# Moving the decay of a linear-attention state from GpSimd to ScalarE, with sums over each head's own columns

## Chip, cores, metric

The kernel runs on one core of one Trainium2 chip. The metric is the device time of one execution in microseconds, as the median of several runs. The engines of the core are TensorE (PE, with its weight loads as PEld), VectorE (DVE), ScalarE (ACT), GpSimd (POOL) and SyncE (SP, which issues the DMAs here).

## What is computed

Three layers one after the other: a gated linear attention, a layer that mixes tokens with cosine and sine of a projection, and a gated convolution layer. The change touches only the first.

```python
B, H, S, D = 4, 8, 768, 48
state = zeros(B, H, D, D)
for t in range(S):
    state = alpha[:, :, t, :, None] * state + einsum('bhd,bhe->bhde', k[:, :, t], v[:, :, t])
    y[:, :, t] = einsum('bhd,bhde->bhe', q[:, :, t], state)
x = y as (B, S, H * D)
theta = x @ w_theta                       # then cos, sin of theta times x, mixed over tokens
u = x + w_tok_r @ (x * cos(theta)) + w_tok_i @ (x * sin(theta))
u = u + relu(u @ w_ch)
h = relu(u @ w_in); out = (h * sigmoid(conv3(h, conv_w))) @ w_out
```

## The kernel before

The recurrence is computed in chunks of 128 tokens, 6 chunks for each of 4 batches, 24 in all (index `ci`, chunk in its batch `c`). Rows of the tiles are head dimensions: two heads lie on one set of partitions, head j of a pair on rows 64j to 64j+47, and the 4 pairs (`NP`) lie side by side.

For each chunk, `a_prep` (L238) makes running products of alpha with two scans on VectorE (L246, L251, into the one buffer `fbt`), copies the total decay of the chunk per row into `ftot` (L254, ScalarE), squares everything for an overflow test (L257, ScalarE, which must have read `fbt` before the next scan may write it) and multiplies queries and keys by the running products (L260, VectorE). `a_score` (L263) transposes the keys (`kps`, TensorE), multiplies keys with queries (`sc`), copies scores to `pt` (L278, ScalarE), masks them (L279, GpSimd) and copies the transposed keys to `kt` (L283, ScalarE). `a_y` (L286) computes the output `y` of the chunk from `pt` and the values, and, for c > 0, from the state `Sp`; ScalarE copies it to `x` (L303). For c < 5 it then computes the outer products `kv` of keys and values over the chunk (L309), adds the old state (L313, VectorE, into `tst`), and multiplies by the total decay `nft` of the next chunk into the other state tile `Sn` (L321, GpSimd, two products, one for each set of rows). For c = 0 there is no old state, and ScalarE copies `kv` instead (L318). `a_xt` transposes x and ScalarE copies it to `u` (L338).

`kv` is computed for a whole pair of heads against the values of both (96 columns), though only the blocks of a head with itself are wanted; the rest is never read, since the products at L321 go over each head's own columns only.

Around this runs other work. Weights come in as 8-byte words and VectorE decodes them (L117 to L119) and splits them (L75). `a_theta` makes cosine and sine (L364 to L369) and splits them into `zh` and `zl`; `m_mix` multiplies them with the token weights (`yps`, TensorE). In the first batch attention, theta and loading run together; the attention of batch b+1 is then woven, chunk by chunk, with the first half of the mixing of batch b, and the theta of batch b+1 with the second half. After the attention of the last batch (about 260 us) come theta, mixing, and the two later layers.

Which instruction an engine issues next is fixed when the program is built: a planner simulates the engines and, on each, puts the instruction first that is ready by its simulation and comes earliest in the program. On the chip each engine then follows that order, whatever is ready. `behind` (L80) adds an order without a wait: the squares are issued behind the score, key, x and u copies made so far.

Of the kernel before, what the change touches and what calls it, by code (L numbers as in the profile page):

```python
# [8 lines left out]
F32 = mybir.dt.float32  # L9
# [5 lines left out]
AF = mybir.ActivationFunctionType  # L15
ALU = mybir.AluOpType
PSUM = bass.MemoryType.PSUM

P = 128
B, H, S, D = 4, 8, 768, 48  # L20
DM = H * D
DFF = 1024
NP = H // 2
# [23 lines left out]
def tile_gated_linear_attention__then__spectral_moe__then__conv_gate(  # L47
# [17 lines left out]
    def mm(o, lhsT, rhs, start, stop):  # L65
        nc.tensor.matmul(o, lhsT, rhs, start=start, stop=stop, skip_group_check=True)  # L66
# [34 lines left out]
    def body(top, slow):  # L101
# [46 lines left out]
        with ExitStack() as ph1:  # L148
# [37 lines left out]

            onehot = acon.tile([P, 5, SEG], BF16, name="onehot")
            starts = acon.tile([P, 4, SEG], F32, name="starts")
            Sst = [acon.tile([P, NP, 2 * D], F32, name=f"S{i}") for i in range(2)]
            magic = acon.tile([P, 1], F32, name="magic")  # L190
            halfpi = acon.tile([P, 1], F32, name="halfpi")
            wth_p = apool("wth", 2, side="right")
# [6 lines left out]
            nc.vector.memset(onehot, 0.0)  # L199
            nc.vector.memset(onehot[:, :, 0:1], 1.0)  # L200
            nc.vector.memset(starts, 0.0)
            for t in Sst:
                nc.gpsimd.memset(t, 0.0)
            nc.gpsimd.memset(magic, MAGIC)
            nc.gpsimd.memset(halfpi, math.pi / 2)

# [31 lines left out]
            def a_prep(ci):  # L238
                at, qt, vt = raw.pop(ci)
                qr = qt[:, 0:CW]  # L240
                kr = qt[:, CW : 2 * CW]
                fbt = sc_p.tile([P, 2 * AW + 6], F32, tag="fbt", name="fbt")
                bf = fbt[:, AW + 1 : 2 * AW + 2]
                of = onehot.rearrange("p a t -> p (a t)")
                ftot = att.tile([P, 4], F32, tag="ftot", name="ftot")
                nc.vector.tensor_tensor_scan(  # L246
                    bf[:, AW:0:-1], at[:, AW:0:-1], of[:, AW:0:-1], 0.0, ALU.mult, ALU.add
                )
                tots = bf[:, 1 : AW + 1].rearrange("p (a t) -> p a t", a=4)[:, :, 0]
                nc.vector.reciprocal(starts[:, :, 0], tots)  # L250
                nc.vector.tensor_tensor_scan(  # L251
                    fbt[:, :AW], at[:, :AW], starts.rearrange("p a t -> p (a t)"), 0.0, ALU.mult, ALU.add
                )
                nc.scalar.copy(ftot, tots)  # L254
                fl = fbt[:, 1 : 2 * AW + 5].rearrange("p (b t) -> p b t", b=2)[:, :, :AW]
                sink = at[:, : AW - 1].bitcast(BF16).rearrange("p (b t) -> p b t", b=2)
                sq = nc.scalar.activation(sink, fl[:, :, : AW - 1], AF.Square, accum_out=bacc[:, ci : ci + 1])  # L257
                behind(sq, ("pt", "kt", "x", "u"))
                q4 = qt.rearrange("p (b a t) -> p b a t", b=2, a=4)
                nc.vector.tensor_tensor(q4, q4, fl.rearrange("p b (a t) -> p b a t", a=4)[:, :, :, :P], ALU.mult)  # L260
                prep[ci] = (qr.rearrange("p (a t) -> p a t", a=4), kr.rearrange("p (a t) -> p a t", a=4), ftot, vt)

            def a_score(ci):  # L263
                qh, kh, ftot, vt = prep[ci]
                kt = None
                if ci % NC < NC - 1:
                    kps = ps_a.tile([P, 4, P], F32, tag="a", name="kps")
                    for p in range(NP):
                        nc.tensor.transpose(kps[:, p, :], kh[:, p, :], ident)
                scs = [ps_a.tile([P, NP, P], F32, tag="a", name="sc") for _ in range(2)]  # L270
                for p in range(NP):
                    for j in range(2):
                        r = slice(64 * j, 64 * j + D)
                        mm(scs[j][:, p, :], kh[r, p, :], qh[r, p, :], True, True)
                pts = []
                for j in range(2):
                    pt = att.tile([P, NP, P], F32, tag="pt", name="pt")
                    marks["pt"] = nc.scalar.copy(pt, scs[j])  # L278
                    nc.gpsimd.affine_select(pt, pt, [[0, NP], [1, P]], ALU.is_ge, 0.0, base=0, channel_multiplier=-1)  # L279
                    pts.append(pt)  # L280
                if ci % NC < NC - 1:
                    kt = att.tile([P, 4, P], F32, tag="kt", name="kt", bufs=1)
                    marks["kt"] = nc.scalar.copy(kt, kps)  # L283
                scored[ci] = (pts, kt)

            def a_y(ci):  # L286
                qh, kh, ftot, vt = prep.pop(ci)
                pts, kt = scored.pop(ci)
                c = ci % NC
                Sp, Sn = Sst[ci % 2], Sst[(ci + 1) % 2]  # L290
                y = ps_a.tile([P, DM], F32, tag="a", name="y")
                halves = [slice(64 * i, 64 * i + 64) for i in range(2)]
                for p in range(NP):
                    for j in range(2):
                        h = 2 * p + j
                        for t in halves:
                            mm(y[t, h * D : (h + 1) * D], pts[j][:, p, t], vt[:, h * D : (h + 1) * D], h == 0, c == 0)
                if c > 0:
                    for p in range(NP):
                        for t in halves:  # L300
                            mm(y[t, p * 96 : p * 96 + 96], qh[:, p, t], Sp[:, p, :], False, True)
                x = x_p.tile([P, DM], F32, tag="x", name="x")
                marks["x"] = nc.scalar.copy(x, y)  # L303
                xs[ci] = x
                if c < NC - 1:
                    kv = ps_a.tile([P, NP, 2 * D], F32, tag="a", name="kv")
                    for p in range(NP):
                        for t in halves:
                            mm(kv[t, p, :], kt[:, p, t], vt[:, p * 96 : p * 96 + 96], p == 0, True)  # L309
                    nft = prep[ci + 1][2]  # L310
                    if c > 0:
                        tt = att.tile([P, NP, 2 * D], F32, tag="tst", name="tst", bufs=1)
                        nc.vector.tensor_tensor(tt[:112], Sp[:112], kv[:112], ALU.add)  # L313
                    else:
                        tt = Sn
                        for j in range(2):
                            r = slice(64 * j, 64 * j + D)
                            nc.scalar.copy(Sn[r, :, j * D : (j + 1) * D], kv[r, :, j * D : (j + 1) * D])  # L318
                    for j in range(2):
                        r = slice(64 * j, 64 * j + D)  # L320
                        nc.gpsimd.tensor_tensor(  # L321
                            Sn[r, :, j * D : (j + 1) * D],
                            tt[r, :, j * D : (j + 1) * D],
                            nft[r].unsqueeze(2).to_broadcast([D, NP, D]),
                            ALU.mult,
                        )

            def a_xt(ci):
                b, c = divmod(ci, NC)
# [407 lines left out]
```

## Time and profile before

| | |
|---|---|
| median of 3 runs | 577.38 us (576.98 to 578.29) |
| profiled execution | 575.62 us |
| its span | 573.9 us |
| TensorE matmuls | 550.9 us busy (96%) |
| TensorE weight loads | 514.3 us (90%) |
| VectorE | 455.1 us (79%) |
| ScalarE | 336.0 us (59%) |
| GpSimd | 90.8 us (16%) |

The span runs from the first to the last instruction of the profiled execution. Busy shares are averages over stages with different limits, so the rows further down are taken stage by stage. A line of code can be that of a helper: all plain matmuls have L66, the splits L74 (the cast, ScalarE) and L75 (the difference, VectorE).

### The profile page before, as it was taken

Reading aid. Unit: us, or ns where it says so; the run is one execution under the profiler, and the core shown is the slowest. Engines: PE = TensorE matmul, PEld = TensorE weight load, DVE = VectorE, ACT = ScalarE, POOL = GpSimd, SP = SyncE. Lnnn points to the kernel's source line nnn. Section 1 sums busy time; section 2 is a strip of 40 time slices with the busy share of each in tenths; the row PEclk is TensorE's granted clock in tenths of the full one; section 3 lists DMA queues with packets and bytes.
Section 4 is the critical chain, followed back from the end, with each engine's and each line's share of the span. In section 5 each row is a group of like instructions: output and inputs, shape, how many; then the busy total and the mean of one; then the engine's idle time right before and its main releaser. Section 6 shows DMA issues by size and latency. Waiting matters only on the chain.

```text
span 573.9 us, 10776 instructions
## 1 busy us (share of the span) xinstructions
PE 550.9 (96%) x4317; PEld 514.3 (90%) x4317; DVE 455.1 (79%) x682; ACT 336.0 (59%) x685; POOL 90.8 (16%) x99
## 2 busy tenths in 40 slices
PE   6888989999999999999999999899999999999996
PEld 3766879877999999999999999799999999999995
DVE  7999998999767674642747999987888888898780
ACT  3566666457844476443742346567767766676661
POOL 2465414440154101440000000000000000000000
PEclk9699999999999999999999999999999999999998
DMA  8556544673044300400013333401053443647001
GB/s 323 182 166 200 189 143 139 203 265 102 15 139 140 125 2 15 140 15 1 1 55 138 111 111 111 164 1 42 14 193 118 145 147 115 198 138 243 17 30 46
DMA packets 25402, 66.59 MB, mean 116 GB/s; under 512 B 2560, under 2 KB 8704, under 8 KB 24960
## 3 DMA queue, kind: packets, MB, share of 16 engines
q1 hardware_dynamic: 25344, 65.82, 34.9%
q8 instruction: 36, 0.59, 0.4%
q14 instruction: 22, 0.18, 0.1%
HBM read 61.10 MB, written 4.72 MB: 115 GB/s over the span
## 4 chain that ended last, share of the span: by engine, by line
PE 70%; DVE 16%; DMA 7%; issue 2%; ACT 2%; POOL 2%; SPq 1%; DVEq 0%; POOLq 0%; ACTq 0%
PE yps L66 18%; PE ops L66 17%; PE hps L66 15%; PE th L66 5%; PE y L66 4%; PE cps L66 3%; PE sc L66 3%; DVE stage L118 2%; DMA stage<-in_w_in_dram 2%; DMA stage<-in_w_tok_dram 2%; DVE stage L117 2%; DVE stage L119 2%; PE kv L66 2%; DMA stage<-in_w_out_dram 1%; DMA stage<-in_w_theta_dram 1%
## 5 line engine op out<-in xcount | busy, mean ns | idle before, releaser
L66 PE MATMUL yps<-wtok,zh 128*128 128x384 f32 x576 | 152.6, 343 | 1.3 <-ACT zh L74 1.3
L66 PEld LDWEIGHTS yps<-wtok,zh 128*128 128x128 f32 x576 | 104.4, 189 | 5.0 <-ACT zh L74 1.6
L66 PE MATMUL hps<-x,win 128*128 128x386 f32 x576 | 107.7, 339 | 0.0
L66 PE MATMUL ops<-wout,g 128*128 128x384 f32 x576 | 106.9, 338 | 0.0
L66 PEld LDWEIGHTS hps<-x,win 128*128 128x128 f32 x576 | 102.3, 189 | 0.4
L66 PEld LDWEIGHTS ops<-wout,g 128*128 128x128 f32 x576 | 101.6, 188 | 0.4
L66 PE MATMUL yps<-wtok,zl 128*128 128x384 f32 x288 | 96.7, 341 | 0.8 <-DVE zl L75 0.8
L279 POOL TENSOR_SCALAR_AFFINE_SELECT pt<-pt 128x512 f32<-128x512 f32 x48 | 55.0, 1166 | 151.1 <-ACT pt L278 151.0
L66 PEld LDWEIGHTS yps<-wtok,zl 128*128 128x128 f32 x288 | 54.3, 189 | 2.0 <-DVE zl L75 1.0
L246 DVE TENSOR_TENSOR_SCAN fbt<-a_t,onehot 128x516 f32<-128x516 f32 x24 | 29.5, 1229 | 23.2 <-ACT a_t L257 21.3
L75 DVE TENSOR_TENSOR g<-cv,g 128x384 fp32r<-128x384 f32 x64 | 35.5, 556 | 12.2 <-ACT g L74 11.2
L561 ACT ACTIVATE cv<-cv 128x384 f32<-128x384 f32 x64 | 33.2, 522 | 20.0 <-DVE cv L558 19.9
L562 DVE SCALAR_TENSOR_TENSOR cv<-cv,hh 128x384 f32<-128x384 f32 x64 | 35.1, 555 | 10.5 <-ACT cv L561 9.0
L552 ACT ACTIVATE cv<-hh,cw 128x384 f32<-128x384 f32 x64 | 38.6, 615 | 5.0 <-DVE g L75 4.9
L66 PE MATMUL cps<-us,wch 128*128 128x512 f32 x162 | 40.0, 396 | 1.5 <-DVE us L75 1.5
L555 DVE SCALAR_TENSOR_TENSOR cv<-hh,cw,cv 128x383 f32<-128x383 f32 (+1 forms) x64 | 38.7, 614 | 3.3 <-ACT cv L552 2.8
L74 ACT CAST g<-cv 128x384 fp32r<-128x384 f32 x64 | 32.6, 510 | 13.6 <-DVE cv L562 12.3
L558 DVE SCALAR_TENSOR_TENSOR cv<-hh,cw,cv 128x384 f32<-128x384 f32 (+1 forms) x64 | 38.8, 615 | 1.0
L66 PEld LDWEIGHTS cps<-us,wch 128*128 128x128 f32 x162 | 30.3, 189 | 8.3 <-DVE us L75 2.4
L550 ACT ACTIVATE hh<-hps 128x386 f32<-128x386 f32 x64 | 31.4, 491 | 10.4 <-PE hps L66 10.3
L260 DVE TENSOR_TENSOR qk_t<-qk_t,fbt 128x1024 f32<-128x1024 f32 x24 | 33.3, 1388 | 0.9
L369 DVE TENSOR_TENSOR zf<-x,zf 128x768 f32<-128x768 f32 x24 | 23.6, 986 | 13.1 <-ACT zf L368 13.1
(90 smaller groups left out, 827.9 us busy)
## 6 DMA issues: line engine op xcount, KB each, us to landing
qk_t<-in_qka_dram SPq DMA_DIRECT2D x24, 512.0 KB, 4.5
stage<-in_w_tok_dram SPq DMA_DIRECT2D x12, 768.0 KB, 4.7
top<-in_w_tok_dram SPq DMA_DIRECT2D x12, 768.0 KB, 4.3
a_t<-in_qka_dram SPq DMA_DIRECT2D x24, 260.0 KB, 2.7
v_t<-in_v_dram SPq DMA_DIRECT2D x24, 192.0 KB, 3.7
out_dram<-ob SPq DMA_DIRECT2D x24, 192.0 KB, 2.0
stage<-in_w_in_dram SPq DMA_DIRECT2D x4, 768.0 KB, 4.3
stage<-in_w_out_dram SPq DMA_DIRECT2D x4, 768.0 KB, 5.0
```

Of the source, the lines that this page charges most:

```text
L66: nc.tensor.matmul(o, lhsT, rhs, start=start, stop=stop, skip_group_check=True)
L74: cast = nc.scalar.copy(hi, src)
L75: lo_eng.tensor_tensor(lo, src, hi.bitcast(F32), ALU.subtract)
L246: nc.vector.tensor_tensor_scan(bf[:, AW:0:-1], at[:, AW:0:-1], of[:, AW:0:-1], 0.0, ALU.mult, ALU.add)
L260: nc.vector.tensor_tensor(q4, q4, fl.rearrange("p b (a t) -> p b a t", a=4)[:, :, :, :P], ALU.mult)
L279: nc.gpsimd.affine_select(pt, pt, [[0, NP], [1, P]], ALU.is_ge, 0.0, base=0, channel_multiplier=-1)
L550: nc.scalar.activation(hh, ps[:, :HW], AF.Relu)
L552: nc.scalar.activation(cv, hh[:, o : o + HALF], AF.Copy, scale=cw[:, f, 1:2])
L555: nc.vector.scalar_tensor_tensor(cv[:, a:HALF], hh[:, o + a - 1 : o + HALF - 1], cw[:, f, 0:1], cv[:, a:HALF], ALU.mult, ALU.add)
L558: nc.vector.scalar_tensor_tensor(cv[:, 0:e], hh[:, o + 1 : o + 1 + e], cw[:, f, 2:3], cv[:, 0:e], ALU.mult, ALU.add)
L561: nc.scalar.activation(cv, cv, AF.Tanh, scale=0.5)
L562: nc.vector.scalar_tensor_tensor(cv, cv, 1.0, hh[:, o : o + HALF], ALU.add, ALU.mult)
```

## The change

There is one state tile `Sst` and one tile of sums `Ssum` instead of two state tiles and `tst`. The outer products `kv` are computed for each head against its own 48 columns of values. The old state is added on VectorE in two instructions, one for each set of rows, over own columns only, into `Ssum` (for c = 0 ScalarE copies `kv` there as before). GpSimd's two products are replaced by four ScalarE activations, one for each pair of heads, that multiply 96 columns of `Ssum` by a factor per row and write `Sst`. `ftot` has 4 buffers instead of 2, `kt` 2 instead of 1. Only `Ssum` is cleared at the start.

```diff
-            Sst = [acon.tile([P, NP, 2 * D], F32, name=f"S{i}") for i in range(2)]
+            Sst = acon.tile([P, NP, 2 * D], F32, name="S")
+            Ssum = acon.tile([P, NP, 2 * D], F32, name="Ssum")
...
-            for t in Sst:
-                nc.gpsimd.memset(t, 0.0)
+            nc.gpsimd.memset(Ssum, 0.0)
...
-                ftot = att.tile([P, 4], F32, tag="ftot", name="ftot")
+                ftot = att.tile([P, 4], F32, tag="ftot", name="ftot", bufs=4)
...
-                    kt = att.tile([P, 4, P], F32, tag="kt", name="kt", bufs=1)
+                    kt = att.tile([P, 4, P], F32, tag="kt", name="kt")
...
-                Sp, Sn = Sst[ci % 2], Sst[(ci + 1) % 2]
...
-                            mm(y[t, p * 96 : p * 96 + 96], qh[:, p, t], Sp[:, p, :], False, True)
+                            mm(y[t, p * 96 : p * 96 + 96], qh[:, p, t], Sst[:, p, :], False, True)
...
-                        for t in halves:
-                            mm(kv[t, p, :], kt[:, p, t], vt[:, p * 96 : p * 96 + 96], p == 0, True)
+                        for j, t in enumerate(halves):
+                            h = 2 * p + j
+                            own = slice(j * D, (j + 1) * D)
+                            mm(kv[t, p, own], kt[:, p, t], vt[:, h * D : (h + 1) * D], p == 0, True)
                     nft = prep[ci + 1][2]
-                    if c > 0:
-                        tt = att.tile([P, NP, 2 * D], F32, tag="tst", name="tst", bufs=1)
-                        nc.vector.tensor_tensor(tt[:112], Sp[:112], kv[:112], ALU.add)
-                    else:
-                        tt = Sn
-                        for j in range(2):
-                            r = slice(64 * j, 64 * j + D)
-                            nc.scalar.copy(Sn[r, :, j * D : (j + 1) * D], kv[r, :, j * D : (j + 1) * D])
                     for j in range(2):
                         r = slice(64 * j, 64 * j + D)
-                        nc.gpsimd.tensor_tensor(
-                            Sn[r, :, j * D : (j + 1) * D],
-                            tt[r, :, j * D : (j + 1) * D],
-                            nft[r].unsqueeze(2).to_broadcast([D, NP, D]),
-                            ALU.mult,
-                        )
+                        own = slice(j * D, (j + 1) * D)
+                        if c > 0:
+                            nc.vector.tensor_tensor(Ssum[r, :, own], Sst[r, :, own], kv[r, :, own], ALU.add)
+                        else:
+                            nc.scalar.copy(Ssum[r, :, own], kv[r, :, own])
+                    for p in range(NP):
+                        nc.scalar.activation(Sst[:, p, :], Ssum[:, p, :], AF.Copy, scale=nft[:, p : p + 1])
```

## Rows read from the trace of the kernel before

**Rows 1.** Busy time by stretch: length, then each engine's busy us (instructions).

```profile
20.00:84.00 64.00, 56.43 (x599) 47.06 (x598) 62.86 (x74) 40.78 (x83) 28.01 (x22) 0.92 0.55 176
84.00:120.00 36.00, 34.68 (x471) 31.62 (x471) 33.98 (x39) 20.65 (x44) 18.21 (x19) 1.00 0.57 182
160.00:190.00 30.00, 30.00 (x426) 28.12 (x423) 21.21 (x26) 15.59 (x36) 14.85 (x17) 1.00 0.49 148
```

**Rows 2.** Waits over the span: engine, for whom; us in total, times, longest.

```profile
ACT ftot L254 <- POOL S L321: 9.0, 3, 3.3
...
PE y L66 <- POOL S L321: 4.1, 4, 2.3
```

**Rows 3.** Timeline of TensorE in a steady chunk: start us, us, instruction, records.

```profile
158.64 1.14 PE L66 MATMUL y<-v_t,pt 128*64 128x48 f32 x32
...
159.61 0.85 PE L66 MATMUL y<-S,qk_t 128*64 128x96 f32 x16
...
160.28 0.83 PE L66 MATMUL kv<-v_t,kt 128*64 128x96 f32 x16
...
161.04 0.62 PE L66 MATMUL yps<-wtok,zh 128*128 128x384 f32 x2
...
164.28 0.60 PE L269 MATMUL kps<-ident,qk_t 128*128 128x128 f32 x4
```

**Rows 4.** Groups of instructions by shape: busy us, mean ns, idle before.

```profile
L552 ACT ACTIVATE cv<-hh,cw 128x384 f32<-128x384 f32 x64 | 38.6, 615 | 5.0 <-DVE g L75 4.9
...
L74 ACT CAST g<-cv 128x384 fp32r<-128x384 f32 x64 | 32.6, 510 | 13.6 <-DVE cv L562 12.3
...
L74 ACT CAST zh<-zf 128x768 fp32r<-128x768 f32 x24 | 20.1, 836 | 10.7 <-DVE zf L369 10.4
...
L75 DVE TENSOR_TENSOR wtok<-stage,wtok 128x768 fp32r<-128x768 f32 x12 | 11.4, 950 | 0.9 <-ACT wtok L74 0.8
```

**Rows 5.** Timeline of VectorE in the same chunk.

```profile
158.87 1.23 DVE L246 TENSOR_TENSOR_SCAN fbt<-a_t,onehot 128x516 f32<-128x516 f32 x1 [1.62 <-ACT a_t L257]
...
160.35 1.23 DVE L251 TENSOR_TENSOR_SCAN fbt<-a_t,starts 128x516 f32<-128x516 f32 x1
161.62 1.47 DVE L260 TENSOR_TENSOR qk_t<-qk_t,fbt 128x1024 f32<-128x1024 f32 x1
163.01 0.54 DVE L313 TENSOR_TENSOR tst<-S,kv 112x384 f32<-112x384 f32 x1
166.05 1.23 DVE L246 TENSOR_TENSOR_SCAN fbt<-a_t,onehot 128x516 f32<-128x516 f32 x1 [2.49 <-ACT a_t L257]
```

**Rows 6.** Timeline of ScalarE in that chunk and the first of its batch.

```profile
157.30 0.48 ACT L338 COPY u<-xps 128x384 f32<-128x384 f32 x1
...
164.48 0.48 ACT L338 COPY u<-xps 128x384 f32<-128x384 f32 x1 [2.26 <-PE xps L337]
164.86 1.06 ACT L257 ACTIVATE a_t<-fbt 128x1030 bf16<-128x1030 f32 x1
```

**Rows 7.** Timeline: a pair of GpSimd's products, and VectorE's instructions beside two pairs.

```profile
49.55 4.54 POOL L321 TENSOR_TENSOR S<-tst,ftot 48x192 f32<-48x192 f32 x2 [1.36 <-DVE tst L313]
...
53.78 1.40 DVE L251 TENSOR_TENSOR_SCAN fbt<-a_t,starts 128x516 f32<-128x516 f32 x1
...
59.47 1.26 DVE L75 TENSOR_TENSOR zl<-zf,zh 128x768 fp32r<-128x768 f32 x1
```

**Rows 8.** Timeline in the second batch's attention, three engines.

```profile
93.00 0.54 DVE L313 TENSOR_TENSOR tst<-S,kv 112x384 f32<-112x384 f32 x1
...
93.98 0.48 ACT L338 COPY u<-xps 128x384 f32<-128x384 f32 x1 [1.77 <-PE xps L337]
...
95.09 1.07 ACT L257 ACTIVATE a_t<-fbt 128x1030 bf16<-128x1030 f32 x1
...
96.28 1.23 DVE L246 TENSOR_TENSOR_SCAN fbt<-a_t,onehot 128x516 f32<-128x516 f32 x1
...
117.61 0.63 PE L269 MATMUL kps<-ident,qk_t 128*128 128x128 f32 x4 [0.32 <-issue]
```

## The prediction

> **What bounds the kernel now.** I read the busy times by stretch first, since the share of the whole span (TensorE 96%) mixes stages. From 20 to 84 us VectorE is busy 62.86 of 64.00 us and TensorE only 56.43; from 84 to 120 both are nearly full (33.98 and 34.68 of 36.00); from 160 to 190 TensorE is busy all 30.00 us and VectorE 21.21 [rows 1]. So the attention is bound by VectorE at first, then by both, then by TensorE. Behind the attention nothing is edited, and the loads of the later layers go into space that the attention frees, so I take a shift of the front to move the end by the same amount.
>
> Second, the list of waits: TensorE waited 4.1 us in all for GpSimd's product into the state, and ScalarE 9.0 us for the same product to let go of a buffer of totals [rows 2]. These look like the prize, but they fall into the first two stretches, where VectorE hardly ever stood idle; what VectorE does decides there, not who waits for GpSimd.
>
> Third, the timelines of one steady chunk (158 to 166 us), engine by engine, for the durations [rows 3, 5, 6].
>
> **The change part by part.** I take each against the profiled execution (span 573.9 us, 575.62 us as timed; the median 577.38 lies 1.76 us above it, and I carry the same shift over to the median).
>
> *kv on own columns only.* Each of the 8 matmuls per chunk (16 records) streams 48 columns instead of 96. The row of the same stationary shape with 48 columns shows 32 records from 158.64 to 159.61, 30.3 ns each; with 96 columns 16 records from 159.61 to 160.28, 41.9 ns each [rows 3]. So 16 x 11.6 = 0.19 us a chunk. (Bounds: 0, if something other than columns set the pace; 0.28, if the 0.76 us from kv to the next matmul [rows 3] fell to 0.48.) There are 20 such chunks; the ten of the third and fourth batch stand on TensorE's full stretch: -1.9 us. The one at 89.8 us counts too (-0.19); the others lie where VectorE decides.
>
> *The add in two halves.* Before: one 112x384 add, 0.54 us [rows 5]. 768 columns take 0.95 us [rows 4], so 192 columns less cost 0.205 us less: 0.335 us a half. Consecutive VectorE instructions overlap by some 0.08 us (161.62 + 1.47 against a next start of 163.01 [rows 5]). Two halves hold the engine 0.51 us if they overlap so, 0.70 us if not at all; the old one held it 0.46. So +0.05 to +0.24 us a chunk; no row shows a VectorE instruction that starts in the middle of the partitions, and I take +0.15. Four adds lie before 84 us (+0.6), three more before 117.6 us (+0.45); the rest is hidden under TensorE.
>
> The Trainium skill (VectorE: DVE Perf Modes, section "Two Vector instructions with no wait between them") says that an instruction whose operands start in another 32-partition group than those before it begins only when every earlier one has finished; the second half starts at partition 64. By that rule the halves would not overlap, and seven adds would cost 0.6 us more than I take; no run here shows it yet.
>
> *GpSimd's products go.* They cost GpSimd much and VectorE a little: the pair at 49.55 took 4.54 us, while the scan beside it took 1.40 us instead of the 1.23 it takes elsewhere, and the subtraction at 59.47 took 1.26 instead of 0.95 [rows 4, 5, 7]. I went through VectorE's timeline beside the first five pairs and summed what its instructions took over their usual time: 0.30, 0.17, 0.17, 0.17 and 0.62 us, together 1.43; beside the pairs at 101 and 110 us it is 0.58. GpSimd's masks of the scores stay and go on slowing VectorE as now.
>
> *Four decays on ScalarE.* No 128x96 row exists. A 128x384 activation with a factor per row takes 0.615 us; 768 against 384 columns differ by 0.326 us [rows 4], so 288 columns less give 0.37 us. Neighbours overlap by 0.10 (0.48 us long, next start after 0.38 [rows 6]), so four hold ScalarE 1.08 us; bounds 1.08 and 1.48. ScalarE has room (40.78 of 64 us, 15.59 of 30 us [rows 1]), but it issues in order. The decays wait for the adds, and queued behind them are the copy u, the squares (L257, which must finish before the next scan may overwrite fbt), the copy of totals and the score copies. Where u comes soon after the add, this costs: the add stands at 93.00, u at 93.98, then a cast and the squares (95.09, with the reading of their sum until 96.2), and the next scan starts at 96.28 right behind them [rows 8]. Decays from 92.94 (all moved by -0.8, below) hold ScalarE until 94.02, where u would have run at 92.98: +1.04 us at that scan.
>
> *Buffers.* Totals 2 to 4 and keys 1 to 2 remove ScalarE waits that lie under a full VectorE: nothing by themselves. The state tile that is now single is rewritten only after the y matmuls that read it, which precede kv on TensorE anyway; the decayed state is wanted about 3.8 us after the add (add at 163.01, next y with S one 7.2 us period after 159.61): nothing.
>
> *Sum.* At 84 us: +0.6 - 1.43 = -0.8. At the scan at 96.28: -0.8 - 0.19 + 1.04 = 0. Then VectorE runs without a pause to the transposes of keys at 117.61 [rows 8]: +0.45 - 0.58 = -0.1. From there TensorE decides: -0.1 - 1.9 = -2.0 us, if the decays stall nothing there. Forecast 575.4 us (574.2 to 576.2: without the delay at 96 us it is -3.0, with unoverlapped halves -1.4).
>
> **The rivals.**
> *(a) A loop over ScalarE and VectorE takes the place of TensorE.* In the steady chunks the add stands behind the product into q and k (L260) though kv was done at 161.04 [rows 3, 5]. If that order stays and the decays stand before u, there is a loop: u 0.38, squares to the next scan 1.19, scan to second scan 1.48, to L260 1.27, to the add 1.39 [rows 5, 6], both halves 0.70, a hand-over 0.04, decays 1.08: 7.53 us. The period now is 7.2 us (166.05 - 158.87), TensorE's after the change 7.0. So each chunk falls behind by 0.53 us; the slack before TensorE notices is 1.19 us (L260 ends at 163.09, key transposes at 164.28 [rows 3, 5]). Third batch: its first chunk already puts 1.08 us of decays before u at 157.30 [rows 6], so 1.08 + 3 x 0.53 - 1.19 = 1.5; fourth batch, where u comes late: 3 x 0.53 - 1.2 = 0.4. Sum -2.0 + 1.9 = -0.1: 577.3 us. Against it: a queue laid out with the highest priority to what is ready would move the add ahead of L260 once VectorE lags, since kv is then long done, and the loop is cut.
> *(b) Slower: the same loop with the dear ends.* Decays at 1.48 us make the loop 7.93 us, 0.93 a chunk: third batch 1.48 + 2.8 - 1.2 = 3.1, fourth 2.8 - 1.2 = 1.6, the delay at 96 us 0.4 more, seven adds 0.6 more: -2.0 + 5.7 = +3.7, 581.1 us. It decides for slower from a loop of some 7.75 us (6 x 0.75 + 1.1 - 2.4 = 3.2 of stalls).
> *(c) More gain.* GpSimd's lateness and the short buffers also set the order in which VectorE got its work. VectorE's whole idle time from 20 to 120 us is 3.2 us [rows 1]; if half of it goes, -3.6 us: 573.8.
> *(d) The narrower kv doesn't run faster* (0 instead of 0.19): -0.1 us, 577.3.
>
> **How the numbers follow.** A measurement of this kernel tells about 0.2% (1.15 us) from no change, so faster is below 576.2, slower above 578.5. Forecast 0.45, (a) 0.27, (b) 0.12, (c) 0.13, (d) 0.03. (a) spreads over 576 to 578.7 with its lag, so it gives 0.02 to faster and 0.01 to slower. Faster 0.45 + 0.13 + 0.02 = 0.60, slower 0.12 + 0.01 = 0.13, same 0.27. The range leaves out most of (b) and the far half of (c): 573.0 to 579.0; the forecast alone 574.2 to 576.2.
>
> **What would show it.** kv at about 30 ns a record; the halves at 0.33 to 0.36 us; decays at 0.37 us, 0.27 apart; the scan L251 back near 1.23 us where GpSimd's products ran; TensorE without waits behind 120 us. Rival (a) or (b) would show as TensorE waiting for L260 (the key transposes or the score matmuls) in the third batch, u starting right behind a decay, and periods between scans above 7.2 us. The prediction is wrong if the queues of the engines came out in another order altogether, or if a decay costs well over 0.37 us.

## The result, and the profile after

The change makes the kernel slower: 580.25 us as the median of 8 runs (578.94 to 583.72) against 576.5 us before (574.98 to 578.29), ratio 1.0067 with a 95% interval of [1.0045, 1.0089], some 3.9 us. 575.4 was forecast, with a range of 573.0 to 579.0: the sign is wrong and the time lies outside the range. The profiled execution of the changed kernel took 583.72 us (span 582.0 us), 3.5 us above its median, so single times below are read against their neighbours, not against the median.

The busy time by stretch (length, then PE, PEld, DVE, ACT and POOL with instructions, the granted clock, DMA):

```profile
20.00:84.00 64.00, 53.89 (x543) 44.74 (x543) 55.25 (x68) 41.17 (x91) 13.58 (x12) 0.88 0.52 164
84.00:120.00 36.00, 33.62 (x470) 31.20 (x468) 33.67 (x43) 25.79 (x60) 10.13 (x8) 0.95 0.47 158
160.00:190.00 30.00, 29.49 (x413) 27.59 (x413) 19.18 (x24) 20.82 (x52) 9.63 (x8) 1.00 0.33 107
```

Against [rows 1], VectorE, which bounds the first stretch, stands idle 8.75 of 64 us where it stood idle 1.14 us, and TensorE is no longer full from 160 to 190 us. ScalarE is busy only two thirds of the first stretch. A second profiled execution of the changed kernel, 2 us faster as a whole, shows the same stretch with VectorE idle 6.92 us:

```profile
20.00:84.00 64.00, 54.15 (x575) 44.98 (x575) 57.08 (x70) 42.56 (x94) 13.44 (x12) 0.88 0.54 170
```

The list of waits names what came in place of [rows 2]; the first two lines are of the whole span, the others up to 84 us:

```profile
ACT S L320 <- DVE Ssum L316: 32.4, 15, 3.2
ACT ftot L254 <- DVE fbt L246: 20.9, 21, 2.8
...
DVE wtok L75 <- ACT wtok L74: 2.9, 2, 2.4
PE kps L269 <- DVE qk_t L260: 2.5, 1, 2.5
DVE fbt L246 <- ACT a_t L257: 2.5, 1, 2.5
...
DVE stage L117 <- DMA stage<-in_w_tok_dram: 2.0, 1, 2.0
```

The waits for GpSimd's product are gone. ScalarE now waits 32.4 us for VectorE's adds (7.2 us of it up to 84 us), and in places VectorE waits for what stands behind that on ScalarE. One such place in full, ScalarE and then VectorE, in the first batch:

```profile
28.07 0.48 ACT L302 COPY x<-y 128x384 f32<-128x384 f32 x1 [0.39 <-PE y L66]
31.79 1.17 ACT L320 ACTIVATE S<-Ssum,ftot 128x96 f32<-128x96 f32 x4 [3.24 <-DVE Ssum L316]
32.87 0.46 ACT L332 COPY u<-xps 128x384 f32<-128x384 f32 x1
33.23 0.83 ACT L74 CAST wtok<-stage 128x768 fp32r<-128x768 f32 x1
33.96 1.06 ACT L257 ACTIVATE a_t<-fbt 128x1030 bf16<-128x1030 f32 x1
```

```profile
29.68 1.38 DVE L119 SCALAR_TENSOR_TENSOR stage<-stage 128x768 uint32<-128x768 uint32 x1
30.99 0.71 DVE L316 TENSOR_TENSOR Ssum<-S,kv 48x192 f32<-48x192 f32 x2
34.09 0.96 DVE L75 TENSOR_TENSOR wtok<-stage,wtok 128x768 fp32r<-128x768 f32 x1 [2.39 <-ACT wtok L74]
35.15 1.23 DVE L246 TENSOR_TENSOR_SCAN fbt<-a_t,onehot 128x516 f32<-128x516 f32 x1
```

ScalarE is idle for 3.24 us and holds behind it the copy u, the cast of the token weights and the squares, none of which needs the state. VectorE's next instruction wants that cast, so it stands 2.39 us until the decays, u and the cast have gone by one after the other.

This is not the whole of VectorE's idle time. After the next add (43.18) the same happens with 0.48 us; after the third (52.95) the decays wait for nothing; before the fourth (65.94) VectorE itself stands 1.96 us for the DMA of the token weights, and the decays wait for that. So of the 8.75 us, 2.87 are waits for the cast behind the decays, 1.96 are the DMA, and 2.49 are a wait for the squares in front of the scan at 23.58, before any add of the batch (the first chunk's decays, which read copies and no add, had held ScalarE 1.08 us ahead of it). The DMA wait is not in the second profiled execution, and a run below whose first batch is that of the kernel before has 1.65 us in front of the same scan.

The steady chunk of the third batch (TensorE, VectorE, ScalarE), to be held against [rows 3, 5, 6]:

```profile
171.77 0.63 PE L269 MATMUL kps<-ident,qk_t 128*128 128x128 f32 x4 [0.40 <-PE xps L331]
...
174.38 0.85 PE L66 MATMUL y<-S,qk_t 128*64 128x96 f32 x16
175.06 0.62 PE L66 MATMUL kv<-v_t,kt 128*64 128x48 f32 x16
175.61 0.44 PE L66 MATMUL yps<-wtok,zh 128*128 128x384 f32 x1
```

```profile
168.93 1.23 DVE L251 TENSOR_TENSOR_SCAN fbt<-a_t,starts 128x516 f32<-128x516 f32 x1
170.20 1.47 DVE L260 TENSOR_TENSOR qk_t<-qk_t,fbt 128x1024 f32<-128x1024 f32 x1
171.59 0.71 DVE L316 TENSOR_TENSOR Ssum<-S,kv 48x192 f32<-48x192 f32 x2
...
175.01 1.23 DVE L246 TENSOR_TENSOR_SCAN fbt<-a_t,onehot 128x516 f32<-128x516 f32 x1 [2.71 <-ACT a_t L257]
```

```profile
172.39 1.17 ACT L320 ACTIVATE S<-Ssum,ftot 128x96 f32<-128x96 f32 x4 [2.13 <-DVE Ssum L316]
173.47 0.45 ACT L332 COPY u<-xps 128x384 f32<-128x384 f32 x1
173.83 1.06 ACT L257 ACTIVATE a_t<-fbt 128x1030 bf16<-128x1030 f32 x1
174.79 0.19 ACT L257 ACTIVATION_READ_ACCUMULATOR a_t<-fbt 128x1 f32 x1
174.89 0.56 ACT L283 COPY kt<-kps 128x512 f32<-128x512 f32 x1
```

kv takes 0.55 us to the next matmul instead of 0.76: 0.21 us less, where 0.19 was forecast. The loop of rival (a) is there link by link: L260, the halves, the decays, u, the squares, the scan. The next L260 starts at 177.76, 7.56 us after this one, where 7.53 was worked out. TensorE stands 0.40 us at the key transposes (171.77); the row names the transposes before them, but those start at 170.88 and take 0.49 us, while L260, which writes what is transposed, ends at 171.67.

### The profile page after: what moved, and what is told of

The parts are those of the page before. It is cut to its first block, busy times and chain, and to the rows that moved or that the text cites. A ratio compares the mean times of both kernels' runs of the same rounds, so it can differ in the third digit from the quotient of the medians.

```text
span 582.0 us, 10813 instructions
## 1 busy us (share of the span) xinstructions
PE 551.7 (95%) x4317; PEld 515.2 (89%) x4317; DVE 455.7 (78%) x698; ACT 356.6 (61%) x765; POOL 57.7 (10%) x58
## 4 chain that ended last, share of the span: by engine, by line
PE 65%; DVE 13%; DMA 4%; ACT 2%; issue 1%; DVEq 0%; POOLq 0%; ACTq 0%
PE ops L66 17%; PE yps L66 16%; PE hps L66 15%; PE th L66 5%; PE y L66 3%; PE cps L66 3%; PE sc L66 2%; DVE stage L118 2%; DMA stage<-in_w_in_dram 2%; DMA stage<-in_w_out_dram 1%; DVE stage L119 1%; DVE stage L117 1%; DVE qk_t L260 1%; DVE fbt L251 1%; DVE fbt L246 1%; PE kv L66 1%
## 5 line engine op out<-in xcount | busy, mean ns | idle before, releaser
L66 PE MATMUL yps<-wtok,zh 128*128 128x384 f32 x576 | 155.7, 346 | 4.9 <-ACT zh L74 4.2
L66 PEld LDWEIGHTS yps<-wtok,zh 128*128 128x128 f32 x576 | 105.7, 191 | 8.1 <-ACT zh L74 4.3
L279 POOL TENSOR_SCALAR_AFFINE_SELECT pt<-pt 128x512 f32<-128x512 f32 x48 | 56.5, 1198 | 204.9 <-ACT pt L278 204.9
L75 DVE TENSOR_TENSOR g<-cv,g 128x384 fp32r<-128x384 f32 x64 | 35.4, 556 | 12.1 <-ACT g L74 11.2
L320 ACT ACTIVATE S<-Ssum,ftot 128x96 f32<-128x96 f32 x80 | 23.4, 363 | 32.5 <-DVE Ssum L316 32.4
L66 PE MATMUL sc<-qk_t 48*128 48x128 f32 x384 | 33.0, 298 | 1.6 <-DVE Ssum L316 0.9
```

Source lines behind the costliest of these rows:

```text
L75: lo_eng.tensor_tensor(lo, src, hi.bitcast(F32), ALU.subtract)
L320: nc.scalar.activation(Sst[:, p, :], Ssum[:, p, :], AF.Copy, scale=nft[:, p : p + 1])
```

## The experiments

Ratios are to the kernel before, run on the same chip in between (not all runs shared one chip); their intervals are 0.0012 to 0.0035 to each side, and a difference of two runs is good to some 0.2 to 0.4% (1.1 to 2.3 us). Besides the time I read from each trace where the ninth L260 (the product into queries and keys, one per chunk) starts: VectorE reaches it at 77.37 us before. In two runs below whose first batch is the code of before it comes at 77.73 and 78.38 us, so a difference of 1 us here says little. From the fourth to the ninth L260 these three traces agree better: 50.20, 50.19 and 50.23 us. The changed kernel was run again beside the first three experiments: 

> The changed kernel as it is, for a second profiled execution (the first lies 3.5 us above the median of its runs). Theory Q (queue: the decays stand in ScalarE's fixed order in front of u, the cast of the token weights and the squares, wait there for VectorE's adds, and VectorE in turn waits for what is queued behind them): 580 us, VectorE idle over 5 us between 20 and 84 us against 1.1 before, third batch's period of the product L260 at 7.5 to 7.7 us. Rival W (the 1.1 us of ScalarE work per chunk costs by itself): same time, but without waits of the decays for the adds. Rival A (the two half adds on VectorE cost): same time, VectorE without idle time, its busy time up.

It gave 1.0072 [1.0052, 1.0092], with the ninth L260 at 82.60 us, 54.40 us behind the fourth.

**The decays, their wait, and their place.** First the decays went back to GpSimd, all else as changed:

```diff
-                    for p in range(NP):
-                        nc.scalar.activation(Sst[:, p, :], Ssum[:, p, :], AF.Copy, scale=nft[:, p : p + 1])
...
+                        nc.gpsimd.tensor_tensor(
+                            Sst[r, :, own], Ssum[r, :, own], nft[r].unsqueeze(2).to_broadcast([D, NP, D]), ALU.mult
+                        )
```

> Undoes one part: the decay is two GpSimd products from the sums into the single state tile again, all else as changed (kv on own columns, two half adds, single state, more buffers). Q and W: the loss goes and the narrower kv shows, 574 to 576 us, 0.995 to 1.000 of before, VectorE idle between 20 and 84 us back under 2 us. A, or a reshuffled order from the buffers: stays at 579 to 581 us.

Measured: 1.0019 [0.9994, 1.0043]. Then the decays stayed on ScalarE, but behind u and the squares of the next chunk:

```diff
+                if c > 0:
+                    for p in range(NP):
+                        d = nc.scalar.activation(Sst[:, p, :], Ssum[:, p, :], AF.Copy, scale=ftot[:, p : p + 1])
+                        behind(d, ("u", "sq"))
...
-                    for p in range(NP):
-                        nc.scalar.activation(Sst[:, p, :], Ssum[:, p, :], AF.Copy, scale=nft[:, p : p + 1])
```

> All instructions as changed, only ScalarE's order: the four decays are issued behind u and behind the next chunk's squares instead of in front of u. Q: VectorE's waits for the cast and the squares go, 575 to 578 us. W: ScalarE has the same work, stays at 579 to 581 us. A: stays at 579 to 581 us. Under Q a rest may show as TensorE waiting for the state, up to 0.3 us for each of 8 chunks behind 150 us.

Measured: 1.0059 [1.0023, 1.0094]. Third, decays of the same size that wait for nothing on VectorE (they read `ident`, the adds sum up in `Ssum`; the recurrence is left out):

```diff
-                            nc.vector.tensor_tensor(Ssum[r, :, own], Sst[r, :, own], kv[r, :, own], ALU.add)
+                            nc.vector.tensor_tensor(Ssum[r, :, own], Ssum[r, :, own], kv[r, :, own], ALU.add)
...
-                        nc.scalar.activation(Sst[:, p, :], Ssum[:, p, :], AF.Copy, scale=nft[:, p : p + 1])
+                        nc.scalar.activation(Sst[:, p, :], ident[:, : 2 * D], AF.Copy, scale=nft[:, p : p + 1])
```

> Leaves out the recurrence of the state: the four activations per chunk run on a constant tile instead of the sums, so they no longer wait for the adds; the adds run on into the sums alone. ScalarE and VectorE have the same instructions. Q: ScalarE never stands still for an add, 574 to 577 us. W: 579 to 581 us, since the work is all there. A: 579 to 581 us.

Measured: 1.0037 [1.0011, 1.0063]. In the first stretch the two runs on ScalarE do what the queue theory says. From 20 to 84 us, run behind the squares first, run without the wait second:

```profile
20.00:84.00 64.00, 56.40 (x597) 46.57 (x597) 60.88 (x76) 44.80 (x100) 11.95 (x12) 0.92 0.55 178
```

```profile
20.00:84.00 64.00, 56.80 (x597) 46.61 (x597) 60.98 (x75) 44.54 (x98) 13.09 (x12) 0.89 0.54 178
```

ScalarE does as much as in the changed kernel or more, and VectorE is busy 3.8 to 3.9 us more than in the changed kernel run again; the ninth L260 starts at 78.50 and 78.97 us instead of 82.60, and 52.25 and 52.73 us behind the fourth instead of 54.40. So in this stretch the wait in front of other work costs, some 2 us, and not ScalarE's work. TensorE's granted clock does not tell these runs apart: from 20 to 40 us, where the 2.39 us are lost, it is 0.76 in both as in the changed kernel (0.83 before).

The total says less: without the wait some 2 us come back, just beyond the error, and behind the squares only 0.7 us, within it. There the second batch lost it again: between the transposes of x of its fourth and fifth chunk 12.86 us pass instead of 8.37 in the kernel before. In that stretch VectorE waits 0.87 us for the DMA of token weights, and TensorE for those weights:

```profile
115.34 0.52 PE L66 MATMUL yps<-wtok,zh 128*128 128x384 f32 x1 [1.54 <-DVE wtok L75]
```

TensorE's granted clock, 1.00 from 100 to 110 us, is 0.78 from 110 to 120, and behind this wait single products take 0.52 us where they took 0.33 before it. Why the weights come late in this order I did not follow up. And decays on GpSimd, the cure of the wait with the least work on ScalarE, still left the ninth L260 at 81.17 us, 53.49 us behind the fourth. So the queue is not the whole of it.

**Early and late batches apart.** From here on the tiles and buffers are those of before, and the work is changed for some chunks alone.

```diff
-                    for p in range(NP):
-                        for t in halves:
-                            mm(kv[t, p, :], kt[:, p, t], vt[:, p * 96 : p * 96 + 96], p == 0, True)
+                    if ci >= 2 * NC:
+                        for p in range(NP):
+                            for j, t in enumerate(halves):
+                                h = 2 * p + j
+                                own = slice(j * D, (j + 1) * D)
+                                mm(kv[t, p, own], kt[:, p, t], vt[:, h * D : (h + 1) * D], p == 0, True)
...
+                                nc.vector.tensor_tensor(tt[r, :, own], Sp[r, :, own], kv[r, :, own], ALU.add)
```

That is narrow outer products and halves in the third and fourth batch, with GpSimd's products. 

> Only the third and fourth batch get the narrow outer products and the adds in halves; the state is still decayed by two GpSimd products there, and the first two batches are as before. If the term of the narrow outer products is right (16 records, 0.21 us less a chunk) and VectorE's adds lie hidden under TensorE in those batches: ten chunks, -2.0 us, ratio 0.9965. If the adds in halves or the order that the planner makes of them cost something there too (theory A): no gain, 1.000 or above.

Measured: 0.9962 [0.9947, 0.9978], 572.89 us: -2.2 us. It has the lowest time of the study, though the next run isn't clear of it. The same with the four decays on ScalarE in those batches:

> As the run above, but with the decays on ScalarE in the third and fourth batch (two state tiles, buffers of totals and keys as before; first two batches as before). If the loop over ScalarE and VectorE (7.5 us a chunk against TensorE's 7.0) decides there, as the periods of the changed kernel say (7.56 to 7.69): 1.5 to 2 us above the run above, about -0.2 us against before, ratio 0.9995. If the loss of the change lies in the first stretch alone and ScalarE has room here: as the run above, 0.9965. If ScalarE's work itself costs wherever it stands (theory W), 10 chunks of 1.1 us partly show: +2 us or more, 1.003.

Measured: 0.9969 [0.9957, 0.9981]. The loop runs there at 7.5 to 7.6 us a chunk (L260 at 163.22, 170.75, 178.38, 186.01), and yet the decays cost 0.4 us (with 1.1 us of uncertainty), not the 1.5 to 2 expected of the loop: from 158 to 205 us TensorE is idle 0.66 of 47 us. The reason is TensorE's own chunk. I had put it at 7.0 us, but its transposes of x in this run come at 157.11, 164.51 and 171.91 us, 7.40 apart (7.27 before): the planner fills what kv gives back with mixing, 18 products of token weights from one transpose of keys to the next where there were 16. So the loop loses 0.1 to 0.2 us a chunk on TensorE, not 0.53. Now the mirror image, all of the change's work in the first two batches (`if ci < 2 * NC`):

> The narrow outer products, the adds in halves and the decays on ScalarE in the first two batches only; the third and fourth batch as before. If the change loses its time where VectorE decides and ScalarE's queue stands waiting for the adds (theory Q): the first chunks are 4 to 6 us late by 90 us, some of it is kept to the end, +3.5 to +5 us, ratio 1.006 to 1.009, that is as much as the whole change or more. If the loss is spread over all chunks: half of it, +2 us, 1.0035.

Measured: 1.0058 [1.0035, 1.0081], ninth L260 at 83.16 us. The loss lies in the first two batches. Without the decays there, that is narrow outer products and halves with GpSimd's products:

> Narrow outer products and adds in halves in the first two batches only, the state decayed by GpSimd's two products, tiles and buffers as before, third and fourth batch as before. If ScalarE's queue behind the adds makes the early loss (theory Q): nearly as before, 0 to +0.5 us, ratio 1.000 to 1.001, where the same with the decays on ScalarE had 1.0058. If the adds in halves and the order that comes with them make it (theory A): +3 us, ratio 1.005, like the run with the decays.

Measured: 1.0030 [1.0016, 1.0045], ninth L260 at 80.33 us. Neither theory had it: halfway between. So the halves alone, with wide outer products:

> In the first two batches only the add in two halves (outer products wide as before, decay by GpSimd's two products, tiles and buffers as before). The narrow outer products and the halves together cost 1.7 us there (1.0030). If VectorE's second instruction makes it, 0.24 us more in each of seven adds or the order that comes of it: as that run, 1.002 to 1.003. If it is the earlier end of the narrow outer products and the order that comes of that: 1.000.

Measured: 1.0060 [1.0040, 1.0079], ninth L260 at 80.51 us, more than I had expected at most. The ninth L260 is 52.55 us behind the fourth, 2.35 more than before. VectorE in one turn of its work from L251 to L251, 11.26 us, where before it is 10.52 us (43.26 to 53.78); L319 is the pair of adds, L325 below GpSimd's products, and L391 the product that is L369 in the kernel before:

```profile
45.56 1.23 DVE L251 TENSOR_TENSOR_SCAN fbt<-a_t,starts 128x516 f32<-128x516 f32 x1
46.83 1.23 DVE L260 TENSOR_TENSOR qk_t<-qk_t,fbt 128x1024 f32<-128x1024 f32 x1
47.97 1.39 DVE L391 TENSOR_TENSOR zf<-x,zf 128x768 f32<-128x768 f32 x1
49.28 0.98 DVE L117 TENSOR_SCALAR stage<-stage 128x768 uint32<-128x768 uint32 x1
50.30 0.96 DVE L118 SCALAR_TENSOR_TENSOR stage<-stage 128x768 uint32<-128x768 uint32 x1
51.17 0.73 DVE L319 TENSOR_TENSOR tst<-S,kv 48x192 f32<-48x192 f32 x2
51.93 0.98 DVE L75 TENSOR_TENSOR zl<-zf,zh 128x768 fp32r<-128x768 f32 x1
52.84 1.26 DVE L119 SCALAR_TENSOR_TENSOR stage<-stage 128x768 uint32<-128x768 uint32 x1
54.02 0.95 DVE L75 TENSOR_TENSOR wtok<-stage,wtok 128x768 fp32r<-128x768 f32 x1
54.89 1.22 DVE L246 TENSOR_TENSOR_SCAN fbt<-a_t,onehot 128x516 f32<-128x516 f32 x1
...
56.82 1.23 DVE L251 TENSOR_TENSOR_SCAN fbt<-a_t,starts 128x516 f32<-128x516 f32 x1
```

The pair holds VectorE 0.76 us (51.17 to 51.93) where the single add held it 0.46: +0.30 us of the 0.74. The rest is other instructions that now meet GpSimd at another point: L391 at 1.39 us beside a mask, where it took 0.95, L119 at 1.26 beside the products, where it took 0.95; L118 and the scan L251 run shorter than before in return (0.96 against 1.27, 1.23 against 1.40). This turn is one of the two dearest: from L260 to L260 the two turns after it are 0.26 us and nothing longer than before.

```profile
47.66 2.19 POOL L279 TENSOR_SCALAR_AFFINE_SELECT pt<-pt 128x512 f32<-128x512 f32 x2 [5.63 <-ACT pt L278]
51.60 1.68 POOL L325 TENSOR_TENSOR S<-tst,ftot 48x192 f32<-48x192 f32 x2 [1.75 <-DVE tst L319]
```

**Tiles and buffers.** Four buffers of totals in the kernel before:

```diff
-                ftot = att.tile([P, 4], F32, tag="ftot", name="ftot")
+                ftot = att.tile([P, 4], F32, tag="ftot", name="ftot", bufs=4)
```

> The kernel before with four buffers of totals instead of two and nothing else. The 9.0 us in which ScalarE waited for GpSimd to let a buffer of totals go are gone from the list of waits. If they lie under a VectorE that is never idle, as the prediction says: no change, 1.000 within 0.001. If the wait kept ScalarE from feeding VectorE, or the planner's order depends on it: up to 2 us either way, 0.9965 to 1.0035.

Measured: 1.0003 [0.9990, 1.0017]. The 9.0 us of ScalarE's waits that had looked like a prize were worth nothing. All tiles and buffers of the changed kernel with the work of before:

```diff
-                Sp, Sn = Sst[ci % 2], Sst[(ci + 1) % 2]
+                Sp, Sn, tt = Sst, Sst, Ssum
...
-                    kt = att.tile([P, 4, P], F32, tag="kt", name="kt", bufs=1)
+                    kt = att.tile([P, 4, P], F32, tag="kt", name="kt")
```

> The work of the kernel before (wide outer products, one add, GpSimd's two products) in the tiles and buffers of the changed kernel: one state tile, one tile of sums, four buffers of totals, two of keys. If tiles and buffers cost nothing, as the prediction says: 1.000 within 0.001. If the single state tile or the order that comes of two key buffers costs (theory L): the changed kernel with GpSimd's decay stood at 1.0019 though its late batches alone gain 2.2 us, so up to +3.3 us, ratio 1.0055, with the first batch late by 3 us or more at 85 us.

Measured: 0.9991 [0.9967, 1.0014]. Alone they are free. But the whole change of the work in the old tiles and buffers,

> The whole change of the work (narrow outer products, adds in halves, four decays on ScalarE) in all chunks, but with two state tiles and the buffers of totals and keys as before. If the early and the late part simply add up: -1.8 and +3.3 us, +1.5 us, ratio 1.0027, and the other 2.6 us of the changed kernel belong to its tiles and buffers (theory L). If they don't add up, because a late front in the first batch makes the later batches lose their gain too: as the changed kernel, 1.007.

gave 1.0012 [0.9995, 1.0028], and with four totals besides,

> The whole change of the work in the old state tiles and with one buffer of keys, but four buffers of totals. If the totals make the difference between 1.0012 and the changed kernel's 1.0067: 1.006. If not: 1.001 to 1.002.

1.0035 [1.0023, 1.0047]; the sum of the late and the early run, 1.0027, lies between. The two differ by the totals alone, 0.0023, at the edge of the error: that four totals cost something beside decays on ScalarE is not excluded. Both are under the changed kernel. What is left is the single state tile and the second key buffer; the changed kernel with that buffer taken back (`bufs=1` in the line above):

> The changed kernel with one buffer of keys as before; one state tile, one tile of sums and four buffers of totals as changed. The change in the old tiles and buffers stood at 1.0012, the changed kernel at 1.0067 to 1.0072. If the second key buffer, or the order that comes of it, makes the difference: 1.001 to 1.002. If the single state tile or the totals make it: 1.006 to 1.007.

Measured: 1.0030 [1.0016, 1.0043]. So the state tile is free (1.0030 against the 1.0035 above), and the second buffer of keys costs about 0.4%, 2.1 to 2.4 us with 1.5 us of uncertainty, in the kernel whose decays stand on ScalarE. The traces show part of how. With one buffer the copy of keys has to wait until kv has read the one before, and the planner puts it behind the copy x; with two it puts it right behind the squares. ScalarE in the third batch with one key buffer:

```profile
173.99 0.19 ACT L257 ACTIVATION_READ_ACCUMULATOR a_t<-fbt 128x1 f32 x1
175.47 0.20 ACT L254 COPY ftot<-fbt 128x4 f32<-128x4 f32 x1 [1.30 <-DVE fbt L246]
175.58 1.07 ACT L278 COPY pt<-sc 128x512 f32<-128x512 f32 x2
176.53 0.49 ACT L302 COPY x<-y 128x384 f32<-128x384 f32 x1
176.90 0.61 ACT L283 COPY kt<-kps 128x512 f32<-128x512 f32 x1
```

The whole order of the woven work shifts with it. With one key buffer L260 ends 1.4 us before the transposes that want its result (TensorE, then VectorE), with two it ends 0.1 us before TensorE goes on:

```profile
171.94 0.49 PE L331 MATMUL xps<-ident,x 128*128 128x128 f32 x3
172.26 0.60 PE L269 MATMUL kps<-ident,qk_t 128*128 128x128 f32 x4
```

```profile
169.39 1.47 DVE L260 TENSOR_TENSOR qk_t<-qk_t,fbt 128x1024 f32<-128x1024 f32 x1
```

ScalarE's loop is as long in both (from an L260 to the fourth after it 30.8 us with one buffer, 30.5 with two). But with the head start of 1.4 us TensorE is busy all 47.00 us from 158 to 205; with two buffers, in the changed kernel, it is not:

```profile
158.00:205.00 47.00, 45.81 (x572) 42.87 (x570) 31.65 (x40) 31.66 (x78) 15.03 (x12) 1.00 0.37 122
```

It holds in the second profiled execution too (45.91 us), and the change in the old tiles, with one key buffer, is again busy all 47.00 us. These 1.2 us are half of the difference. Another 0.6 us is there by the first transposes of x of the second batch (91.51 us in the changed kernel run again, 90.86 with one key buffer), but that is less than two traces of the same first batch differ; the remainder I can't place. Last, the change in the late batches only, in the new tiles and buffers:

> The change of the work (narrow outer products, halves, decays on ScalarE) in the third and fourth batch only, in the tiles and buffers of the changed kernel; the first two batches do the work of before in those tiles, and GpSimd clears the tile of sums once between. The same in the old tiles stood at 0.9969, the tiles alone at 0.9991. If the parts add up: 0.996 to 0.997. If the new tiles and buffers make ScalarE's loop bite in the third batch (its periods of L260 go to 7.6 us as in the changed kernel and TensorE waits): 0.999 to 1.001.

Measured: 0.9986 [0.9973, 0.9999], with TensorE idle 0.78 us from 158 to 205; the same in the old tiles was idle 0.66 us at 0.9969. So the late half alone doesn't show the stall at its full size; it takes the early half too. That this is because the early half sets the order in which the third batch is entered is my reading, and no run shows it.

The parts as differences of ratios, in us at 576:

| part | from | us | uncertainty |
|---|---|---|---|
| narrow kv and halves, late batches | 0.9962 | -2.2 | 0.9 |
| decays on ScalarE, late | 0.9969 - 0.9962 | +0.4 | 1.1 |
| halves, early | 1.0060 | +3.5 | 1.1 |
| narrow kv, early | 1.0030 - 1.0060 | -1.7 | 1.4 |
| decays from GpSimd to ScalarE, early | 1.0058 - 1.0030 | +1.6 | 1.6 |
| second key buffer | 1.0067 - 1.0030 | +2.1 | 1.5 |
| state tile, totals | 0.9991 and 1.0003 | 0 | 1.4 |
| sum | | +3.7 | |

The changed kernel stands at +3.9. The sum proves less than it seems to. The first five rows add up to the late run and the early run (0.9969 and 1.0058), and the key buffer's row is taken from the changed kernel itself; so what it tests is that late and early together (1.0027) give the changed kernel with one key buffer (1.0030). The same work in the old tiles, at 1.0012, lies 0.9 us under that sum, within the error. What holds is the order of size of the larger parts.

## Why the prediction was wrong

The step that failed is the first two batches. Up to the key transposes at 117.61 us the sum had -0.1 us; the change in those batches alone measures +3.3 us (1.0058). The gain booked behind them came out (-1.8 us, 0.9969, against -1.9), until the second key buffer took it back. Term by term:

**kv: right in size, too little in place.** 0.21 us a chunk against 0.19, and -2.2 us in the late batches against -1.9. That the early ones but one gain nothing, since VectorE decides there, fell: there the runs give -1.7 us, with an uncertainty nearly as large. By what path it gains there is open; no run tells.

**The halves: mis-sized, and the largest error in the first stretch.** The instruction's own length was nearly right (0.35 us against 0.335). I took +0.15 us a chunk, between full overlap and none, with an upper bound of 0.24; it is +0.28 to 0.30. There is no overlap at all, neither between the halves nor with the instruction behind them: in the turn above L75 starts 0.03 us after the pair's end. The rule of the Trainium skill that I had set beside the sum (VectorE: DVE Perf Modes, section "Two Vector instructions with no wait between them": a start in another 32-partition group than the last operands had is held until everything before has finished) says both, since the following instruction starts at partition 0 again. The trace agrees with it, with 0.76 us for two adds of 0.35. And seven adds at +0.30 would make 2.1 of the 3.5 us. The rest is shown only in part: in the turn above other instructions meet GpSimd's at another point, and over the whole span VectorE is busy 457.8 us instead of 455.1, of which eight pairs of 0.70 us for eight adds of 0.54 explain 1.3. The prediction had no term for that.

**GpSimd's products go, decays come: wrong sign.** I booked -2.0 us for contention that ends and +1.04 us at one single place, since "ScalarE has room"; the runs give +1.6 us early and +0.4 late, with uncertainties of 1.6 and 1.1, and undoing this step alone in the changed kernel gave back 3.0 us (1.0072 to 1.0019), with 1.9 of uncertainty. The contention did end: over the span VectorE is busy 455.7 and 456.1 us in the two profiles of the changed kernel, and 459.1 us with the decays back on GpSimd. But what that freed went into waiting. The decays themselves are as forecast: 0.36 us, four in 1.17. But room (ScalarE is busy 41.17 of 64 us) does not help where the order is fixed. Their wait for the adds stands in front of u, the cast of the token weights and the squares in the first batch, where VectorE's adds come late because VectorE is full, and full VectorE is what those three feed: 2.39 and 0.48 us of waits for the cast at two of the four adds, and some 2 us from the fourth to the ninth L260 when the wait is taken out. I looked for this loop in the third and fourth batch, as rival (a), and at 96 us, and did not look at the first batch, where the same links stand with the weight decoding in between. My list of what is queued behind the decays had u, the squares and the copies, and not the cast for which VectorE then waits.

**Buffers: taken as nothing, +2.1 us.** For state and sums that holds, and for the totals in the kernel before. For the keys I argued that a wait that lies under a full VectorE is worth nothing, and that is not the question: a buffer more lets the planner move the copy, and with it the order.

**Rival (a)** had the loop right (7.56 us against 7.53) and its price in the late batches too high, since TensorE's chunk is 7.40 us and not 7.0: 0.4 us in the old tiles, some 1.2 us of idle TensorE in the changed kernel. Its sum of -0.1 us was far from the result, since it was built on the same first stretch as my forecast. Rival (b) named slower, but by decays that hold ScalarE 1.48 us, and they hold it 1.08 (31.79 to 32.87): that it named the sign is luck.

That a shift of the front moves the end by the same amount held to within 1.6 us: in the profile of the changed kernel run again the transposes of x of the last chunk come 6.4 us later than before, its last matmuls 4.8 us, and its span ends 6.0 us later.

## What to carry to other kernels

Before moving a step to an engine "with room", list what stands behind it in that engine's order and who feeds on that; a step that waits for the bounding engine must not stand in front of work that the bounding engine needs. A change can be right for one stage and wrong for another of the same kernel: here the narrow products pay 2.2 us where TensorE decides, and the kernel that makes them in those batches alone, with the decay left on GpSimd, has the lowest time found (572.89 us, 0.9962). And where a planner fixes the order, an extra buffer is a change of order, to be priced as one.

## What the runs showed of the hardware

The time of GpSimd's pair of products depends on what it meets. In the kernel before it takes 4.54 us from 49.55 [rows 7], beside VectorE instructions that keep their 0.95 us, with only the scan at the end at 1.40 instead of 1.23:

```profile
50.25 0.95 DVE L119 SCALAR_TENSOR_TENSOR stage<-stage 128x768 uint32<-128x768 uint32 x1
```

The same two products take 1.68 us in the run with early halves, and there it is L119 on VectorE that takes 1.26 us. In the third batch, where VectorE has less to do, the pair takes 1.08 us. So in these two alignments it was once GpSimd and once VectorE that yielded, and a price read in one doesn't carry over to the other.
